# Local attention scores on TensorE as 64x64 products instead of 128x128 ones, with a new order of steps

## The chip, the cores and the metric

One core of a Trainium2 chip. The metric is device time in microseconds of one execution; the lower the better. TensorE is called PE here, VectorE DVE, ScalarE ACT, GpSimd POOL and SyncE SP, as in the profile. SP issues all loads and stores of this kernel.

## What is computed

Attention over 2 batches of 8 heads, 768 positions and 64 channels, then two feed-forward layers on the 1536 tokens of 512 channels, all in float32.

```python
k_sum = k.reshape(B, H, nb, block, D).max(axis=3)          # block = 32, nb = 24
v_sum = v.reshape(B, H, nb, block, D).mean(axis=3)
mask_l = np.abs(pos[:, None] - pos[None, :]) < window      # window = 16
scores_s = scale * np.einsum('bhsd,bhnd->bhsn', q, k_sum) + np.log(block)
scores_l_m = np.where(mask_l, scale * q @ k.T, -1000000000.0)
a = softmax over concatenate([scores_l_m, scores_s], axis=-1)
x = a @ np.concatenate([v, v_sum], axis=2)
x = np.maximum(x @ w_in, 0.0) ** 2 @ w_out
h = x @ w_in2
out = np.where(h >= 1, h, np.where(h <= -1, 0.0, (h + 1) ** 2 / 4)) @ w_out2
```

A query of the local part sees only the keys within 15 positions, so a tile of 64 queries needs 96 keys around it and the 24 block maxima: 120 columns of scores.

## The kernel before

**Attention** is cut into 24 units. A unit i is a chunk of 256 positions (6 chunks, 3 per batch) and a pair of heads (4 pairs); `geo` (line 301) gives them. Its steps have one letter each in the written order: S the scores on PE (`s_mm`, line 337), M the mask added to them and the minimum of the negated sums (`s_max`, 344, on DVE), E the exponentials (`s_exp`, 353, ACT), R the reciprocal of the sums (`s_inv`, 359), N the product with it (`s_norm`, 364, POOL or DVE), T the transpose on PE (`t_mm`, 368), "to" its way out of PSUM (`t_out`, 373), O the product with v (`o_mm`, 376), oh and ol the high and low part of the result (`o_hi`, `o_lo`), which fill `xh` and `xl`, the input of the feed-forward part.

S of a unit is 4 products of 128 rows and 128 columns. The rows are the channels of both heads; q is loaded into a tile with zeros in the other head's places, and one product takes 128 weight columns of it, 64 queries of each head, at every fourth element (`bass.ds(j, 128, step=4)`). The moving side is a tile `kw` of 24 block maxima, 8 empty columns and 96 keys, four times (for the 4 tiles of 64 queries). For the first 4 units `kw_band` (327) copies the keys into it out of `kp`; for the other 20 SP loads it ready-made (`kw_load`, 321), and `kw_sum` (333) copies the block maxima that `k_sum` (324) made on DVE. The fills of lines 456 to 462 clear the empty parts of kw, q and vw.

```python
PE.matmul(ps[:, j * 128:(j + 1) * 128], qs[cc % 2][:, p, bass.ds(j, 128, step=4)],
          kw[i % NW][:, j, :], start=True, stop=True)
```

The block means of v for batch 0 are products on PE (v0 to v2, vc, vj: `v_sum0`, `v_copy0`, `v_join0`, lines 402 to 413) of a table of weights with v, both loaded by `vn_load` (437); for batch 1 DVE adds them (`v_sum1`).

**Feed-forward.** The 16 weight slices of each layer come as packed 64-bit numbers of 512 KB per half (wl, `w_load`, line 128) and are decoded into a high and a low part by steps on ACT, DVE and POOL (dl, dq, dr, ds, dt, da, wh, wo; lines 132 to 162). A unit of this part is one slice of 128 hidden channels for one tile of tokens: H (`h_mm`, 186) is 12 products into PSUM, ha, hh, hl the activation and its split into high and low, Y (`y_mm`, 225) 12 products more, yo the way out. The first 24 units take tiles of 256 tokens, so that they can begin when a part of the attention is done; the other 84 take 512.

**Order.** Each engine runs its instructions in the order of the program and waits only for what an instruction needs. That order is written out by hand in a string of steps (`PLAN`, line 83): all of attention, the 24 small units, and the decoding up to weight half 15. After it a loop (line 484) takes the rest in a regular order, from unit 24 (`UA`) on: activation of unit u+1, H of u+2, Y of u, one weight half decoded.

Of the kernel before, what the change touches and what calls it, by code (L numbers as in the profile page):

```python
# [43 lines left out]
KW = QT + 2 * WIN  # L44
NGRP = NCH * NP
# [7 lines left out]
CONST_W = M_OFF + 6 * 128  # L53
SUM_W = 6 * 32 + NB
# [23 lines left out]
Y0 M8 N6g E8 wl3 da4 ks9 wo4g S9 kwl11 vs0 M9 E7 R7 N7g kl6 wl5 vl2 wo1v O4 oh4v ol4 T6 to6a ks11 R8 dq3 dr3 S10 E9 O5
oh5v N8g kwl12 ol5 H1 ha1 R9 O6 T7 to7a vp0 M10 S11 E10 oh6v ol6 O7 T8 ds3 dt3 kl7 N9g hh1v dl3 da3 M11 E11 oh7v ol7
H2 to8v T9 ha2 R11 O8 oh8a kl4 km4 H3 hh2a to9a hl1g ol8 O9 kwl13 R10 N10g kwl14 ks12 kl5 km5 wl6 H4 dq6 wh3v dq5 hl2v  # L80
ha4 wo3v Y1 dr6 N11v kwl15 dl5 Y2 ql3 T10 S12 H6 hh4a oh9a ol9 dr5 ds5 km6 ks14 to10a O10 ks13 T11 dl6 dt5 wh5a wl7
M12 S13 da5 wo5v oh10v ha3 hh3a ds6 dt6 da6 wh6v dq7 ol10 H5 hl3v bl1 M13 vs1 to11a O11 oh11a ol11 wl8 vl3 ql4 hl4g
dr7 Y3 ha6 hh6v ha5 S14 kwl18 M14 wo6g Y4 H7 km7 ks15 vp1 vf3 E12 R12 N12g ds7 dl7 E14 kwl16 E13 R13 N13g hh5v S15 M15
T12 dt7 H8 da7 hl6v Y6 dl8 ha8 to12a H10 kwl17 ks16 E15 R15 kwl19 T13 O12 wl9 oh12a wh7v wo7v hl5g N15v R14 to13v ha7
S16 ol12 M16 Y5 yo5 ks17 N14v kwl20 hh7v hl7g H9 ha9 T14 to14v hh9v S17 hh8v E16 R16 hl8v H11 O13 T15 M17 ks18 hl9v
oh13v vl4 S18 ol13 to15v O14 ql5 ha11 M18 ks19 oh14v ol14 kwl22 N16g T16 dq8 vf4 kwl21 ha10 E17 R17 Y7 N17v E18 to16v
O15 oh15v R18 Y8 Y9 dq9 dr9 T17 N18g hh10a ol15 O16 dr8 ds8 S19 vl5 M19 E19 dl9 oh16v kwl23 H12 hl10g Y10 to17v T18
# [9 lines left out]
"""  # L97


def build(tc, qd, kd, kwd, vw, vn, vb, wd, cd, out):  # L100
    nc = tc.nc
    V, A, G, PE, SY = nc.vector, nc.scalar, nc.gpsimd, nc.tensor, nc.sync

# [3 lines left out]
    with tc.tile_pool(name="main", bufs=1) as mp, tc.tile_pool(name="ps", bufs=1, space=PSUM) as pp:  # L107
# [213 lines left out]
        def kw_load(i):  # L321
            SY.dma_start(kw[i % NW], kwd[i - NP])
# [287 lines left out]
```

## Time and profile before

| | us |
|---|---|
| median of 3 runs (lowest to highest) | 627.0 (626.37 to 631.27) |
| the profiled execution | 630.58 |
| its span, first to last instruction | 628.8 |

The profiled execution is one of its own; what is said of single instructions comes from it. Its mean granted clock of PE is 0.992 of full speed. Busy shares of an engine say how long it had an instruction in it, not that it could not have done more. A matmul in fp32 stands in the trace as two records, each with its own weight load (PEld); records overlap, so the time of a group is read from the start of one group to the start of the next.

### The profile page before, as it was taken

How to read it: one execution, taken by the hardware profiler on the slowest of the kernel's cores; microseconds unless marked ns; L12 is line 12 of the kernel's file. 1: busy time of each engine (PE TensorE's matmuls, PEld its weight loads, DVE VectorE, ACT ScalarE, POOL GpSimd, SP SyncE). 2: the span in 40 equal slices, each digit the busy share in tenths (PEclk: the TensorE clock that was granted, in tenths of full speed). 3: DMA queues.
4: the chain of work that ended last, by engine and by line, in shares of the span. 5: the costliest groups of instructions: out<-in, count | busy, mean ns of one | idle time of the engine just before them, and what ended most of it. 6: DMA issues, size and time to landing. Idle time of an engine off the chain costs nothing.

```text
span 628.8 us, 9073 instructions
## 1 busy us (share of the span) xinstructions
PE 612.2 (97%) x3301; PEld 521.1 (83%) x3301; DVE 353.9 (56%) x806; ACT 309.9 (49%) x674; POOL 271.4 (43%) x225
## 2 busy tenths in 40 slices
PE   7789899999999999999999999999999999999997
PEld 5488899999888888888888888888888888888886
DVE  7787767557555545545457665443555545653343
ACT  3866476476564444444354555554544354432221
POOL 4353231246542331343155666554655565552211
PEclk8898999999999999999999999999999999999999
DMA  8999956412321211132022213211222211100111
GB/s 293 295 220 262 237 141 162 127 35 70 104 87 48 96 67 35 67 102 68 33 68 67 68 34 102 66 61 40 68 67 68 70 67 68 33 1 0 68 67 68
DMA packets 20765, 58.13 MB, mean 92 GB/s; under 512 B 2416, under 2 KB 5968, under 8 KB 19952
## 3 DMA queue, kind: packets, MB, share of 16 engines
q1 hardware_dynamic: 20720, 57.55, 31.1%
q8 instruction: 26, 0.43, 0.3%
q14 instruction: 19, 0.16, 0.1%
HBM read 53.65 MB, written 3.15 MB: 90 GB/s over the span
## 4 chain that ended last, share of the span: by engine, by line
PE 74%; DVE 0%; issue 0%
PE bank L198 37%; PE bank L237 35%; PE bank L519 2%; DVE acc L523 0%
## 5 line engine op out<-in xcount | busy, mean ns | idle before, releaser
L149 POOL TENSOR_TENSOR fr<-fx,fr 128x512 uint32<-128x512 uint32 x64 | 83.3, 1302 | 186.7 <-DVE fx L146 172.4
L198 PE MATMUL bank<-xh,wh 128*128 128x512 f32 (+1 forms) x432 | 156.2, 369 | 0.0
L198 PE MATMUL bank<-xl,wh 128*128 128x512 f32 (+1 forms) x432 | 155.0, 366 | 0.3 <-DVE xl L395 0.3
L222 POOL TENSOR_TENSOR gl<-tb,gh 128x512 fp32r<-128x512 f32 (+1 forms) x62 | 72.6, 1171 | 101.4 <-ACT gh L218 77.5
L198 PE MATMUL bank<-xh,wl 128*128 128x512 f32 (+1 forms) x432 | 105.2, 365 | 0.0
L198 PEld LDWEIGHTS bank<-xl,wh 128*128 128x128 f32 x432 | 81.5, 189 | 13.6 <-DVE xl L395 0.5
L198 PEld LDWEIGHTS bank<-xh,wh 128*128 128x128 f32 x432 | 81.5, 189 | 13.4
L198 PEld LDWEIGHTS bank<-xh,wl 128*128 128x128 f32 x432 | 76.3, 189 | 13.1
L159 ACT CAST wh<-fx 128x512 fp32r<-128x512 f32 x57 | 35.4, 621 | 98.0 <-DVE fx L146 96.6
L162 POOL TENSOR_TENSOR wl<-fr,wh 128x512 fp32r<-128x512 f32 x58 | 76.1, 1312 | 5.8 <-ACT wh L159 0.9
L215 DVE CAST gh<-tb 128x512 fp32r<-128x512 f32 (+1 forms) x49 | 24.4, 501 | 93.5 <-ACT tb L207 88.8
L237 PE MATMUL bank<-gh,wh 128*128 128x512 f32 (+1 forms) x240 | 62.3, 351 | 0.5 <-DVE wh L159 0.5
L237 PE MATMUL bank<-gl,wh 128*128 128x512 f32 (+1 forms) x240 | 61.5, 348 | 0.6 <-DVE gl L222 0.5
L206 ACT ACTIVATE ta<-bank 128x512 f32<-128x512 f32 (+1 forms) x60 | 30.6, 510 | 63.6 <-PE bank L198 63.6
L237 PE MATMUL bank<-gh,wl 128*128 128x512 f32 (+1 forms) x240 | 61.1, 346 | 0.0
L210 ACT ACTIVATE ta<-ta,bias 128x512 f32<-128x512 f32 x48 | 34.8, 724 | 49.6 <-DVE ta L209 49.6
L209 DVE TENSOR_SCALAR ta<-bank 128x512 f32<-128x512 f32 x48 | 33.0, 687 | 44.1 <-PE bank L198 44.1
L142 DVE TENSOR_SCALAR fx<-fx 128x512 f32<-128x512 f32 x64 | 29.7, 465 | 45.9 <-ACT fx L140 45.6
L218 ACT CAST gh<-tb 128x512 fp32r<-128x512 f32 x48 | 29.9, 624 | 49.7 <-DVE tb L217 49.7
L341 PE MATMUL bank<-kw,q 128*128 128x128 f32 x192 | 49.3, 409 | 4.9 <-DMA q<-in_qd_dram 4.6
L217 DVE SCALAR_TENSOR_TENSOR tb<-bank,ta 128x512 f32<-128x512 f32 x48 | 33.1, 690 | 34.7 <-ACT ta L210 17.4
L237 PE MATMUL bank<-wh,gh 128*128 128x512 f32 x176 | 52.4, 389 | 0.0
(75 smaller groups left out, 985.5 us busy)
## 6 DMA issues: line engine op xcount, KB each, us to landing
raw<-in_wd_dram SPq DMA_DIRECT2D x64, 512.0 KB
kw<-in_kwd_dram SPq DMA_DIRECT2D x20, 256.0 KB
vw<-in_vw_dram SPq DMA_DIRECT2D x6, 768.0 KB
k<-in_kd_dram SPq DMA_DIRECT2D x8, 400.0 KB
q<-in_qd_dram SPq DMA_DIRECT2D x12, 256.0 KB
out_dram<-acc SPq DMA_DIRECT2D x11, 256.0 KB
acc<-in_vb_dram SPq DMA_DIRECT2D x2, 768.0 KB
acc<-in_vn_dram SPq DMA_DIRECT2D x2, 512.0 KB
```

Of the source, the lines that this page charges most:

```text
L149: G.tensor_tensor(fr[n % NDEC], fx[n % NDEC], fr[n % NDEC], ALU.add)
L159: cp(e)(w_part(wh, n), f32(fx[n % NDEC]))
L162: e.tensor_tensor(w_part(wl, n), f32(fr[n % NDEC]), f32(w_part(wh, n)), ALU.subtract)
L198: PE.matmul(h, a, b, start=i == 0, stop=i == len(ops) - 1)
L206: A.activation(a, h, AF.Relu)
L209: V.tensor_scalar(a, h, -1.0, 1.0, ALU.max, ALU.min)
L210: A.activation(a, a, AF.Square, bias=bias[:, 1:2], scale=0.5)
L217: V.scalar_tensor_tensor(b, h_bank(n), 1.0, a, ALU.max, ALU.mult)
L218: A.copy(hi, b)
L222: e.tensor_tensor(lo, b, f32(hi), ALU.subtract)
L237: PE.matmul(ys[j], a, b, start=f == 0 and i == 0 and (tw == 512 or j % 2 == 0), stop=f == GF - 1 and i == 2 and (tw == 512 or j % 2 == 1))
L341: PE.matmul(ps[:, j * 128:(j + 1) * 128], qs[cc % 2][:, p, bass.ds(j, 128, step=4)], kw[i % NW][:, j, :], start=True, stop=True)
```

## The change

- **Scores.** q is loaded dense, keys are read where they lie in `kp` and block maxima in `ks`; there is no kw any more. A unit is 16 products in fp32: for each of two halves t, 4 products with 96 keys and 4 with 24 maxima, one for each head h (rows 0 to 63 or 64 to 127 of the array) and query tile r (columns 0 to 63 or 64 to 127). The two heads write different PSUM banks (`sbank`). A unit's scores are 120 columns wide instead of 128: keys first, then maxima.
- **Constants and buffers.** Three masks of 128 columns instead of six, all 8 k tiles stay in place (4 buffers before), v has a third buffer in `acc`.
- **Block means of v, batch 0.** 12 products of 96 rows out of the v tiles themselves; the table is 128x96 numbers.
- **PSUM.** Small units from 12 on write their H into banks 4 and 3 in turn; Y of small tiles uses banks 2 and 3 for t = 1 alone.
- **Order.** A new string of steps, which goes four units further (the loop begins at unit 28) and decodes up to weight half 18.

```diff
+KN = KW + NB
...
-CONST_W = M_OFF + 6 * 128
-SUM_W = 6 * 32 + NB
+CONST_W = M_OFF + 3 * 128
+Z_W, SUM_W = 64, 96
...
-kl1 kb1a ql0 kl0 kb0a km1 ks1 warm11 km0 ks0 kl3 km3 ks3 kb3v cl0 S1 M1 E1 kl2 kb2v wl0 S0 wl1 km2 S3 nl2 ks2 S2 R1
+kl1 ql0 warm11 km1 S1 cl0 M1 E1 kl3 km3 S3 wl1 dl1 kl0 km0 S0 dq1 dr1 ql1 M3 S5 ds1 kl2 km2 R1 N1g wl0 dt1 da1 dl0 T1
...
-                ybank[m, g, t] = [bank[2 * (t % 2) + j // 2][:, j % 2 * CH:(j % 2 + 1) * CH] for j in range(4)]
+                ybank[m, g, t] = [bank[2 * (t == 1) + j // 2][:, j % 2 * CH:(j % 2 + 1) * CH] for j in range(4)]
...
         def h_bank(n):
+            if n < 3 * GF:
+                return bank[4][:, n % 2 * CH:(n % 2 + 1) * CH]
             if U[n][3] == CH:
-                return bank[4][:, n % 2 * CH:(n % 2 + 1) * CH]
+                return bank[4 - n % 2][:, :CH]
             return bank[4 + n % 2]
...
-        NK, NW, NS, NPT = 4, 4, 4, 3
+        NK, NS, NPT = B * NP, 4, 3
         cst = av.tile([128, CONST_W], F32, name="cst")
-        qs = [at.tile([128, NP, 2 * CH], F32, name=f"q{i}") for i in range(2)]
+        qs = [at.tile([128, NP, CH], F32, name=f"q{i}") for i in range(2)]
...
-        kw = [at.tile([128, 4, 128], F32, name=f"kw{i}") for i in range(NW)]
...
+        vwt.append(acc[:, 2048:4096].rearrange("p (j n) -> p j n", j=4))
+        vwt += [vwt[0], vwt[1], vwt[0]]
...
+        def sbank(i, j):
+
+            if i < 8:
+                b = ((5, 1), (2, 3))[i % 2][j // 2]
+                c0 = CH * (b != 5)
+            else:
+                b = (5, 2 if i < 10 or i > 15 else 6)[j // 2]
+                c0 = CH * (i % 2 or b == 6)
+            c0 += j % 2 * 128
+            return bank[b][:, c0:c0 + KN]
...
         def q_load(cc):
-            for hf in range(2):
-                SY.dma_start(qs[cc % 2][hf * 64:hf * 64 + 64, :, hf * CH:(hf + 1) * CH], qd[cc, hf])
+            SY.dma_start(qs[cc % 2], qd[cc])

         def v_load(cc):
-            SY.dma_start(vwt[cc % 2][32:128], vw[cc])
+            SY.dma_start(vwt[cc][:KW], vw[cc])
...
-        def kw_load(i):
-            SY.dma_start(kw[i % NW], kwd[i - NP])
...
-        def kw_band(i, e=A):
+        def s_mm(i):
+
             cc, p, c, n = geo(i)
-            base = kp[n % NK][:, c * CH:c * CH + KW]
-            cp(e)(kw[i % NW][:, :, 32:128], bass.AP(base.tensor, base.offset, [list(base.ap[0]), [QT, 4], [1, KW]]))
-
-        def kw_sum(i):
+            for t in range(2):
+                for keys in (True, False):
+                    for h in range(2):
+                        for r in range(2):
+                            j, rows = 2 * t + r, slice(h * 64, h * 64 + 64)
+                            k0 = c * CH + j * QT
+                            b = kp[n % NK][rows, k0:k0 + KW] if keys else ks[n][rows]
+                            PE.matmul(sbank(i, 2 * h + t)[r * 64:r * 64 + 64, 0 if keys else KW:KW if keys else KN],
+                                      qs[cc % 2][rows, p, j * QT:(j + 1) * QT], b, start=True, stop=True)
...
-                PE.matmul(ps[:, j * 128:(j + 1) * 128], qs[cc % 2][:, p, bass.ds(j, 128, step=4)],
-                          kw[i % NW][:, j, :], start=True, stop=True)
...
-                m0 = M_OFF + (c + j) * 128
-                V.tensor_tensor_reduce(s[:, j, :], ps[:, j * 128:(j + 1) * 128], cst[:, m0:m0 + 128],
+                m0 = M_OFF + (0 if (c, j % 2) == (0, 0) else 2 if (c, j % 2) == (CPB - 1, 1) else 1) * 128
+                V.tensor_tensor_reduce(s[:, j, :KN], sbank(i, j), cst[:, m0:m0 + KN],
                                        -SCALE, 3.0e38, ALU.add, ALU.min, st[:, j:j + 1])
...
-                    rs = slice(hf * 64, hf * 64 + 64)
-                    PE.matmul(ps[rs, j * QT:(j + 1) * QT], vwt[cc % 2][:, j, p * 128 + hf * 64:p * 128 + hf * 64 + 64],
-                              pt[i % NPT][:, j, rs], start=True, stop=True)
+                    rs, r0 = slice(hf * 64, hf * 64 + 64), j % 2 * QT
+                    PE.matmul(ps[rs, j * QT:(j + 1) * QT], vwt[cc][:KN, j, p * 128 + hf * 64:p * 128 + hf * 64 + 64],
+                              pt[i % NPT][:KN, 2 * hf + j // 2, r0:r0 + QT], start=True, stop=True)
...
-            for c in (2 * k, 2 * k + 1):
-                rs = slice(c % 4 * 32, c % 4 * 32 + 32)
-                PE.matmul(bank[0][rs], vx[:, c * 32:(c + 1) * 32], vx[:, SUM_W + c * 512:SUM_W + (c + 1) * 512],
-                          start=c < 4, stop=c >= 2)
+            for j in range(4):
+                b0 = NB - 8 * k - 2 * j
+                PE.matmul(bank[0][j * 32:j * 32 + 32], vx[:KW, b0:b0 + 32], vwt[k][:KW, j], start=k == 0, stop=k == 2)
...
-        for w in kw:
-            G.memset(w[:, :, 0:32], 0.0)
-        for q in qs:
-            for hf in range(2):
-                (V if q is qs[0] else G).memset(q[hf * 64:hf * 64 + 64, :, (1 - hf) * CH:(2 - hf) * CH], 0.0)
-        for w in vwt:
-            G.memset(w[:32], 0.0)
...
-        nd = nl = 4 * GF
-        h_mm(UA + 1)
+        nd, nl = 5 * GF - 1, 5 * GF - 2
+        h_mm(UA + GF + 1)
         last = len(U) - GF
-        for u in range(UA, last):
+        for u in range(UA + GF, last):
...
-    qd = q.reshape(B, NP, 2, CPB, 4, QT, D).transpose(0, 3, 2, 6, 1, 5, 4)
-    qd = np.ascontiguousarray(qd.reshape(NCH, 2, D, NP, CH))
+    qd = q.reshape(B, NP, 2, CPB, CH, D).transpose(0, 3, 2, 5, 1, 4)
+    qd = np.ascontiguousarray(qd.reshape(NCH, 2 * D, NP, CH))
```

How the instructions stand now. The first place is PE in the first third of the attention, around the second chunk's score units. Names are tiles with a running number; L341 and L348 are the score products, L382 and L390 the products with v, L371 and L379 the transposes. Before:

```order
L382 MATMUL bank_64<-pt_132,vw_134 64x64 x8
L371 MATMUL bank_70<-cst,s_129 128x128 x4
L341 MATMUL bank_68<-kw_124,q_110 128x128 x4
L382 MATMUL bank_65<-pt_133,vw_134 64x64 x8
L341 MATMUL bank_68<-kw_125,q_110 128x128 x4
L382 MATMUL bank_66<-pt_131,vw_134 64x64 x8
L371 MATMUL bank_70<-cst,s_127 128x128 x4
L341 MATMUL bank_68<-kw_126,q_110 128x128 x4
```

After:

```order
L390 MATMUL bank_66<-pt_131,vw_134 64x64 x8
L390 MATMUL bank_65<-pt_133,vw_134 64x64 x8
L379 MATMUL bank_70<-cst,s_127 120x128 x4
L348 MATMUL bank_68<-k_111,q_109 64x96 x2
L348 MATMUL bank_65<-k_111,q_109 64x96 x2
L348 MATMUL bank_68<-ks_119,q_109 64x24 x2
L348 MATMUL bank_65<-ks_119,q_109 64x24 x2
L348 MATMUL bank_68<-k_111,q_109 64x96 x2
L348 MATMUL bank_65<-k_111,q_109 64x96 x2
L348 MATMUL bank_68<-ks_119,q_109 64x24 x2
L348 MATMUL bank_65<-ks_119,q_109 64x24 x2
L390 MATMUL bank_69<-pt_132,vw_135 64x64 x8
```

A row of 4 products with kw became 8 rows of 2 products each: keys into two banks, maxima into the same two, and once more for the other half; "x2" are the two query tiles of one head.

The second place is the beginning of SP's queue, where all loads are issued (raw is a weight half, vn the table of block means with v, cst the constants). Before:

```order
L308 DMA k_112<-in_kd_dram 128x800
L312 DMA q_109<-in_qd_dram 64x4x256 x2
L308 DMA k_111<-in_kd_dram 128x800
L308 DMA k_114<-in_kd_dram 128x800
L434 DMA cst<-in_cd_dram 128x640
L308 DMA k_113<-in_kd_dram 128x800
L130 DMA raw_74<-in_wd_dram 128x1024
L130 DMA raw_75<-in_wd_dram 128x1024
L438 DMA acc<-in_vn_dram 128x1024
L438 DMA acc<-in_vn_dram 128x1240
L438 DMA acc<-in_vn_dram 128x1024
L322 DMA kw_123<-in_kwd_dram 128x512
```

After:

```order
L325 DMA q_109<-in_qd_dram 128x1024
L441 DMA cst<-in_cd_dram 128x384
L322 DMA k_114<-in_kd_dram 128x800
L131 DMA raw_75<-in_wd_dram 128x1024
L322 DMA k_111<-in_kd_dram 128x800
L325 DMA q_110<-in_qd_dram 128x1024
L322 DMA k_113<-in_kd_dram 128x800
L131 DMA raw_74<-in_wd_dram 128x1024
L328 DMA vw_134<-in_vw_dram 96x2048
L444 DMA acc<-in_vn_dram 128x96
L328 DMA vw_135<-in_vw_dram 96x2048
L328 DMA acc<-in_vw_dram 96x2048
```

The three loads of vn and the loads of kw are gone, q comes in one load, and vw stands three times in the first thirteen places (the third one, the last row, writes acc).

The third place is DVE at the program's start (L325 and L335 of after are the block maxima, L335 and L331 of before the copies into kw). Before:

```order
L460 MEMSET q_109 64x4x256 x2
L325 TENSOR_REDUCE ks_116<-k_112 128x24
L335 COPY kw_124<-ks_116 128x4x24
L325 TENSOR_REDUCE ks_115<-k_111 128x24
L335 COPY kw_123<-ks_115 128x4x24
L325 TENSOR_REDUCE ks_118<-k_114 128x24
L335 COPY kw_126<-ks_118 128x4x24
L331 COPY kw_126<-k_114 128x4x96
```

After:

```order
L297 MEMSET acc 128x256
L335 TENSOR_REDUCE ks_120<-k_112 128x24
L357 ISA s_128,sm_139<-bank_65,cst 128x120
L357 ISA sm_139 128x1
L357 ISA s_128,sm_139<-bank_65,cst 128x120
L357 ISA sm_139 128x1
```

Between a block maximum and the first score no copy stands any more.

## Rows read from the trace of the kernel before

**Rows 1.** The page, busy time, share of the span and instructions of each engine

```profile
PE 612.2 (97%) x3301; PEld 521.1 (83%) x3301; DVE 353.9 (56%) x806; ACT 309.9 (49%) x674; POOL 271.4 (43%) x225
```

**Rows 2.** Four stretches: us, busy time (instructions) by engine, clock, DMA share, GB/s

```profile
0.00:25.00 25.00, 17.48 (x85) 11.38 (x85) 18.26 (x64) 13.30 (x44) 9.96 (x16) 0.93 0.95 284
25.00:80.00 55.00, 49.83 (x421) 46.02 (x422) 42.91 (x159) 32.73 (x108) 22.41 (x20) 0.94 0.98 250
80.00:164.20 84.20, 83.46 (x736) 80.44 (x735) 54.57 (x190) 55.01 (x179) 33.14 (x31) 1.00 0.38 108
164.20:628.80 464.60, 461.44 (x2064) 383.22 (x2063) 238.11 (x394) 208.82 (x345) 205.91 (x159) 1.00 0.19 61
```

**Rows 3.** The chain that ended last, from 176 us: start us, us, what

```profile
176.69 2.72 PE bank L237 x12
179.41 2.72 PE bank L198 x12
```

**Rows 4.** What PE waited for: us in total, times, longest us

```profile
PE bank L341 <- DMA q<-in_qd_dram: 4.6, 3, 2.3
PE bank L371 <- POOL s L366: 2.0, 2, 1.4
PE bank L382 <- DMA vw<-in_vw_dram: 1.5, 1, 1.5
...
PE bank L382 <- DMA vw<-vs: 0.6, 1, 0.6
```

**Rows 5.** Groups of lines on PE: names, shapes, count | busy us, mean ns

```profile
L341 PE MATMUL bank<-kw,q 128*128 128x128 f32 x192 | 49.3, 409 | 4.9 <-DMA q<-in_qd_dram 4.6 <-DVE sm L350 0.3
L341 PEld LDWEIGHTS bank<-kw,q 128*128 128x128 f32 x192 | 46.5, 327 | 6.4 <-issue 2.8 <-DMA q<-in_qd_dram 1.4 <-ACT pt L374 1.1
...
L382 PE MATMUL bank<-pt,vw 128*64 128x64 f32 x384 | 17.3, 236 | 3.2 <-DMA vw<-in_vw_dram 1.5 <-DVE vw L417 1.1 <-DMA vw<-vs 0.6
...
L371 PEld LDWEIGHTS bank<-cst,s 128*128 128x128 f32 x96 | 11.2, 148 | 4.0 <-POOL s L366 2.4 <-DVE fx L142 0.8
...
L413 PE MATMUL bank<-acc 128*24 128x512 f32 x2 | 1.0, 601 | 0.7 <-ACT acc L410 0.7
```

**Rows 6.** PE in order of time, 0 to 60 us: start us, us, what

```profile
8.00 7.84 PE L341 MATMUL bank<-kw,q 128*128 128x128 f32 x32 [2.35 <-DMA q<-in_qd_dram]
...
18.24 1.91 PE L406 MATMUL bank<-acc 128*32 128x512 f32 x12
20.86 1.04 PE L413 MATMUL bank<-acc 128*24 128x512 f32 x2 [0.72 <-ACT acc L410]
...
40.27 2.02 PE L341 MATMUL bank<-kw,q 128*128 128x128 f32 x8
42.12 0.60 PE L371 MATMUL bank<-cst,s 128*128 128x128 f32 x4
...
54.18 0.69 PE L382 MATMUL bank<-pt,vw 128*64 128x64 f32 x16
54.79 0.66 PE L371 MATMUL bank<-cst,s 128*128 128x128 f32 x4
```

**Rows 7.** Groups of lines on DVE, by busy time

```profile
L146 DVE SCALAR_TENSOR_TENSOR fx<-raw,fx 128x512 uint32<-128x512 uint32 x64 | 46.1, 720 | 2.0
...
L144 DVE TENSOR_SCALAR fx<-fx 128x512 uint32<-128x512 uint32 x64 | 30.5, 477 | 1.9
...
L142 DVE TENSOR_SCALAR fx<-fx 128x512 f32<-128x512 f32 x64 | 29.7, 465 | 45.9 <-ACT fx L140 45.6
...
L335 DVE COPY kw<-ks 128x96 f32<-128x96 f32 x24 | 7.4, 314 | 6.4 <-DMA kw<-in_kwd_dram 6.0
```

**Rows 8.** DMA issues: names, count, KB each

```profile
kw<-in_kwd_dram SPq DMA_DIRECT2D x20, 256.0 KB
...
acc<-in_vn_dram SPq DMA_DIRECT2D x2, 512.0 KB
acc<-in_vn_dram SPq DMA_DIRECT2D x1, 620.0 KB
```

More of the change, by code (lines that the diff above doesn't have):

```diff
@@ L78 @@
[L78 to L87, printed above, removed]
@@ L97, with build @@
+hh23a hl23v dt15 wh15a wl18 Y22 wl17 ds16 dt16 wh16a H27 ha27 hh27a Y23 yo23 hl24g H26 ha26 hh26v hl26g Y24 Y25 hl27g
+da16 wo16v da15 wo15v dl18 dq18 dr18 dl17 Y26 ds18 dq17 dr17 dt18 da18 H28 wl19 ds17 dt17 wl20 da17 ha28 Y27 hh28v
+hl28v wh17a wo17g wl21
 """
-def build(tc, qd, kd, kwd, vw, vn, vb, wd, cd, out):
+def build(tc, qd, kd, vw, vn, vb, wd, cd, out):
     nc = tc.nc
@@ L259, in y_out @@
                     A.copy(av[:, :, t % 2 * CH:(t % 2 + 1) * CH],
-                           bank[2 * (t % 2) + j // 2].rearrange("p (j n) -> p j n", j=2))
+                           bank[2 * (t == 1) + j // 2].rearrange("p (j n) -> p j n", j=2))
                 return
@@ L303, in abank @@
         def abank(kind, i):
-            first = {"s": (5, 1, 2, 3), "t": (7, 6, 7, 5), "o": (6, 1, 2, 3)}
-            return bank[first[kind][i] if i < 4 else {"s": 5, "t": 7, "o": 6}[kind]]
+            first = {"t": (7, 6, 7, 5), "o": (6, 1, 2, 3)}[kind]
+            return bank[first[i] if i < len(first) else {"t": 7, "o": 6}[kind]]
+        def sbank(i, j):
[7 more added lines that the diff above has]
+            return bank[b][:, c0:c0 + KN]
         def k_load(n):
@@ L412, in v_join0 @@
         def v_join0(_):
-            PE.matmul(bank[0][:NB], vx[:, 6 * 32:SUM_W], vq, start=True, stop=True)
+            PE.matmul(bank[0][KW:KN], vx[:, Z_W:Z_W + NB], vq, start=True, stop=True)
         def v_fill0(p, e):
@@ L558, in host @@
             vw[cc, :, j] = vt[b, s0:s0 + KW]
-            kw[cc, :, :, j, 32:] = kd[b * NP:(b + 1) * NP, :, s0:s0 + KW]
-    kw = kw.reshape(NGRP, 2 * D, 512)[NP:]
-    vn = np.zeros((128, SUM_W + 6 * H * D), v.dtype)
-    for s in range(S):
-        vn[s % 128, s // 128 * 32 + s // BLK] = 1.0 / BLK
+    vn = np.zeros((128, SUM_W), v.dtype)
     for p in range(128):
+        if 0 <= p - WIN < QT:
+            vn[p, NB + (p - WIN) // BLK] = 1.0 / BLK
         if p % 32 < NB:
-            vn[p, 6 * 32 + p % 32] = 1.0
-    vn[:, SUM_W:] = vt[0, WIN:WIN + S].reshape(6, 128, H * D).transpose(1, 0, 2).reshape(128, -1)
+            vn[p, Z_W + p % 32] = 1.0
     vb = v[1].reshape(2, 4, NB, BLK, D).transpose(0, 1, 2, 4, 3)
@@ L582, in consts @@
     c[:, I_OFF:I_OFF + 128] = np.eye(128, dtype=np.float32)
-    qi = np.arange(128)[:, None] % QT
+    qi = np.arange(QT)[:, None]
     w = np.arange(KW)[None, :]
     band = np.abs(qi - (w - WIN)) < WIN
-    for i in range(6):
-        ok = band & ((w >= WIN) | (i > 0)) & ((w < KW - WIN) | (i < 5))
-        m = c[:, M_OFF + i * 128:M_OFF + (i + 1) * 128]
-        m[:, :NB] = np.log(BLK) / SCALE
-        m[:, NB:32] = NEG
-        m[:, 32:] = np.where(ok, 0.0, NEG)
+    for i in range(3):
+        for r in range(2):
+            ok = band & ((w >= WIN) | ((i, r) != (0, 0))) & ((w < KW - WIN) | ((i, r) != (2, 1)))
+            m = c[r * QT:(r + 1) * QT, M_OFF + i * 128:M_OFF + i * 128 + KN]
+            m[:, :KW] = np.where(ok, 0.0, NEG)
+            m[:, KW:] = np.log(BLK) / SCALE
     return c
```

72 lines of the change are left out of this document (36 added, 36 removed).

## The prediction

> **What bounds the kernel now.** Read the engines' share first [rows 1]: TensorE (PE) is busy 97% of the span, VectorE (DVE) 56%, ScalarE 49%. A busy matmul engine can still be one that waits inside its work, so the stretches come next [rows 2]. There the run has two parts. From 164.2 us to the end PE is busy 461.4 of 464.6 us, and the chain of waits shows why nothing else matters there [rows 3]: groups of 12 products of 512 columns follow each other every 2.72 us, product after product, without a wait. One unit of the feed-forward part costs two such groups, 5.44 us, and the change leaves the number of these units and of their products alone. So this part is a constant, and the time is decided by the moment at which PE gets there. In the first 164.2 us PE is busy 17.5 of 25, 49.8 of 55 and 83.5 of 84.2 us: it idles for 13.4 us, nearly all of it before 80 us, where the DMA queues are full (0.95 and 0.98 of their time) and DVE is busy 42.9 of 55 us. Who PE waited for there is in the table of waits [rows 4]: q loads 4.6 us, loads of vw 1.5 and 0.6 us, 2.0 us for the normalised scores of GpSimd (POOL), the rest under 1.5 us each.
>
> The groups of lines tell what fills PE in the front part [rows 5]. The 192 records of the score products (line 341) hold 49.3 us, more than any other attention line, although the 96 transposes of line 371 move the same 128 columns against weights of the same 128x128 shape. The difference stands in the weight loads: 327 ns each for line 341, 148 for line 371. Line 341 takes its weights from q at every fourth element. In order of time [rows 6] a score unit of 8 records begins at 40.27 and the next group at 42.12, 1.85 us or 231 ns per record, while the 4 transposes that follow take 0.60 us with all of their last record, at most 150 ns per record. PE spends more than half of a score unit on loading weights slowly.
>
> **The change part by part.** *Score products.* Removed: 24 units of 4 products of 128x128, 24 x 1.85 = 44.4 us. Added: 24 units of 16 products, each with 64 rows and 64 weight columns: 8 over 96 keys and 8 over 24 block maxima, in two halves of 4 + 4, one product per quarter of the array. q now lies dense. No row shows products on half of the rows, so the cost is bounded. Two rows give the parts. The two records of line 413 (512 columns, fp32) take 1.04 us [rows 6] with 0.60 for the last [rows 5], so 0.44 us per 512 columns, 0.86 ns a column: 96 keys are 0.083 us per record, and a product has two records. The 16 records of line 382 (64 weight columns, two products side by side on the two column halves) take 0.69 us [rows 6] with 0.24 for one [rows 5], so 15 steps in 0.45 us: 30 ns each, or 0.060 us per record on its own half; the next group starts 0.61 us after the first record, so the last record and the change-over to another shape of the array cost 0.61 - 0.45 = 0.16 us. Hence, for a unit:
> - four at a time: per half 2 x 0.083 for the keys and 2 x 0.060 for the maxima, 0.286; two halves 0.57; with the change-over 0.73 us.
> - at the pace of line 382, 30 ns for each of 32 records: 0.96 + 0.16 = 1.12 us.
> - two at a time (column halves side by side, row halves in turn): twice 0.57, with the change-over 1.30 us.
> - one at a time: four times 0.57, with the change-over 2.45 us, more than before.
>
> I take 0.92, the middle of the first two: line 382 is the nearest row, and it shows that products on separate parts of the array do run side by side. Saving 24 x (1.85 - 0.92) = 22.3 us; ends 26.9 (0.73) and -14.4 (2.45).
>
> What a page says of this pace stands apart. The Trainium skill, TensorE: Matmul & The Clock Gate, section "Wait — 56ns, not 53.3ns?", says that starts of matmuls never come closer than about 25 ns, however few columns they have. The trace's closest steady pace is the 30 ns above. By the page's figure a unit would be an estimated 32 x 0.025 + 0.16 = 0.96 us and the sum below 1.0 us longer; by the row's 30 ns it would be 4.8 us longer.
>
> *Copies and loads that go.* The 24 copies of block maxima into kw on DVE (7.4 us), 4 copies of key bands and 10 fills go [rows 7], as do 20 loads of kw (256 KB) and three of vn (512, 512, 620 KB) against one small one [rows 8]: 6.9 MB of the 20.9 MB that the queues move in the first 80 us (284 GB/s over 25 us, 250 over 55) [rows 2]. At those rates that is some 25 us of queue time, taken out of the stretch where the queues are full. q arrives in one load of whole rows instead of two. PE's waits for loads in this part are 4.6 + 1.5 + 0.6 = 6.7 us [rows 4]. The bounds are 0 and -6.7; I count half, -3.4, because the first loads (k, q, before 8.00 us [rows 6]) can't come earlier and because two vw loads now stand earlier in the queue.
>
> *Block sums of v.* Before: 6 products of 128 rows and 512 columns, 12 records in 1.91 us [rows 6]. Now 12 products of 96 rows, 4 column quarters at a time: 3 rounds of 2 records of 0.44 us, 2.6 us. +0.7 us (0 to +1.9), and PE has to have three vw loads instead of the vn loads.
>
> *Start.* The four first score units run from 8.00 us on for 7.84 us [rows 6], with the first transposes right behind them. When they shrink to 3.7 us, PE gets to the transposes early and waits for the first unit's maximum, exponentials, reciprocal and POOL's product, so part of their saving (4 x 0.93 = 3.7) turns into a wait. I count half as lost: +2.0 (0 to +3.7). The granted clock is 0.93 and 0.94 of full speed in the first two stretches and 1.00 behind them [rows 2], some 1.8 + 3.3 = 5 us of clock lost; a PE that waits more at the start could lose more of it, and I leave this term at 0 with the same loss once more, +5, as its end.
>
> *The order.* Steps of four more feed-forward units now stand in the written order, and three more weight tiles are decoded ahead of the loop (3 x (465 + 477 + 720) ns = 5.0 us of DVE [rows 7]). PE's products in these units are the same and PE has no idle time behind 164.2 us [rows 2], so this is worth 0 as long as PE's queue hides it. Ends: 0 if hidden, +5.0 if DVE is late by all of it.
>
> *Narrower tiles.* Maxima, exponentials and products of scores work on 120 instead of 128 columns. They lie beside PE's work and count 0.
>
> Sum: -22.3 - 3.4 + 0.7 + 2.0 = -23.0 us. The profiled execution took 630.6 us (span 628.8 and 1.8 around it) and would take 607.6; it lies 3.6 us over the median of the runs, 627.0. Against the median the forecast is 627.0 - 23.0 = 604, and I write 603.5 because the DMA term is the one more likely to be larger.
>
> **The rivals.**
> 1. *The row halves don't overlap.* A unit costs 1.30 us; the saving is 24 x 0.55 = 13.2, and with the other terms (4 x 0.55 / 2 at the start) 627.0 - 13.2 - 3.4 + 0.7 + 1.1 = 612. For it: no product of this kernel has used half the rows. Against it: the halves write different PSUM banks, and the column halves of line 382 do overlap.
> 2. *DVE becomes the bound of the front part.* From 25 to 164.2 us DVE is busy 42.9 + 54.6 = 97.5 us [rows 2]. Less the copies of kw behind 25 us (about 5.5) and plus the decoding (5.0) it is 97. With 23 us gone from PE that has to fit into 116 us, a share of 84%; between 25 and 80 us DVE reached 78%. If 78% is what its waits allow, 97 / 0.78 = 124 us are needed, 8 us more: 612. For it: DVE is the fullest of the others just where PE idles. Against it: the order hands copies to ScalarE and POOL, which are under 60%.
> 3. *The quarters run one after another, the kernel gets slower.* Every product holds the array alone: 2.45 us per unit, 24 x 0.60 = 14.4 us more on PE, less 3.4 for the loads, plus 0.7: 639. It decides from 1.85 + 2.7 / 24 = 1.96 us per unit on, that is when the 16 products take more than 0.12 us each. For it: 64 loads and products per unit instead of 16, and an array that changes its shape twice per unit. Against it: line 382.
>
> The Trainium skill speaks to this one: TensorEngine Tiling (Array Packing), section "Gotcha 1: PSUM Pressure", says that different row tiles can't reach the same PSUM bank at once. No row here shows it; the new placing has the row halves in different banks, so by that rule one reason for rivals 1 and 3 is gone; at the lower end that this leaves, 0.73 us per unit, the sum would give 599.
>
> **How the numbers follow.** Forecast 0.70, rival 1 0.14, rival 2 0.10, rival 3 0.06. The forecast's own range is from 596 (0.73 us per unit, nothing lost at the start: 627.0 - 26.9 - 3.4 + 0.7 = 597, and a little more of the waits for loads gone) to 610 (1.12 us: 604 + 24 x 0.20, and the rest of the start, 1.7). Rivals 1 and 2 at 612, with 3 or 4 us of their own, are taken in: 596 to 616; rival 3 and some of the tails stay out. About 1% (6 us) is what a measurement of this kernel tells from no change. Forecast, rival 1 and most of rival 2 are faster by more than that: 0.91. Rival 2 with all its terms on the bad side, or rival 3 between 1.7 and 2.2 us per unit, is no change: 0.05. The rest of rival 3 is slower: 0.04.
>
> **What would show it.** Right: the start of the steady groups of 2.72 us moves from about 164 to about 141 us; a score unit starts its next group 0.7 to 1.1 us after its own first record; the dense weight loads are far under 327 ns; PE's waits for q and vw shrink and the share of the queues in the first 80 us falls under 0.9; the stretch behind the front lasts as long as before. Wrong: score units at 1.3 us or more (rival 1, from 1.96 on rival 3); idle time of PE between 25 and 140 us released by DVE or ScalarE that is larger than now (rival 2); a gap in the steady part, which would mean that the moved decoding was not hidden.

## The result, and the profile after

| | before | after |
|---|---|---|
| median of 4 runs (lowest to highest), us | 627.7 (626.37 to 631.27) | 607.71 (605.38 to 608.92) |
| the profiled execution, us | 630.58 | 605.38 |
| its span, us | 628.8 | 603.5 |

After stands to before as 0.967, 95% interval 0.962 to 0.972: 20 us less by the medians. The two profiled executions lie 25.2 us apart, because that of before is among its slowest runs and that of after is its fastest; a sum read from the one trace has to be held against the other, so against 25.2.

The page of after, busy time and share of the span of each engine, against [rows 1]:

```profile
PE 589.2 (98%) x3889; PEld 493.4 (82%) x3889; DVE 345.4 (57%) x779; ACT 309.1 (51%) x672; POOL 262.5 (43%) x214
```

The stretches of after (us, busy time by engine with instructions, clock, DMA share, GB/s), the third cut where the steady groups were forecast to begin, and the chain of waits of after behind it:

```profile
0.00:25.00 25.00, 17.80 (x227) 10.51 (x231) 14.74 (x71) 12.22 (x47) 4.29 (x8) 0.70 0.94 280
25.00:80.00 55.00, 51.17 (x818) 44.10 (x814) 47.78 (x169) 44.19 (x147) 29.64 (x28) 0.98 0.71 211
80.00:141.00 61.00, 61.00 (x801) 57.91 (x796) 46.53 (x153) 44.50 (x136) 22.60 (x20) 1.00 0.23 72
141.00:603.50 462.50, 459.18 (x2057) 380.89 (x2056) 236.36 (x389) 208.22 (x344) 205.98 (x160) 1.00 0.18 61
```

```profile
161.53 2.72 PE bank L201 x12
164.25 2.72 PE bank L240 x12
```

Set beside [rows 2, 3], the back part is the same: groups of 2.72 us, PE busy 459 of 462.5 us. The first product of unit 31 stands 25.4 us earlier than before, and so does that of the last unit (587.73 against 613.09 us). All of the gain was made before that. The first product of unit 30 stands at 195.57 us before and at 169.53 after, 26.0 us earlier, of which 0.7 is lost again up to unit 31. Up to unit 30 (before, then after):

```profile
0.00:195.57 195.57, 182.15 (x1394) 164.52 (x1394) 133.20 (x441) 118.13 (x359) 80.06 (x77) 0.97 0.60 167
```

```profile
0.00:169.53 169.53, 158.50 (x1982) 137.07 (x1982) 123.60 (x411) 116.18 (x355) 69.73 (x66) 0.95 0.49 150
```

PE's busy time fell by 23.7 us and its idle time by 2.4 (13.4 to 11.0). What it waits for has changed more. PE's table of waits of after (us in total, times, longest us):

```profile
PE bank L379 <- POOL s L374: 2.0, 2, 1.6
PE bank L348 <- DVE sm L357: 1.8, 2, 1.1
PE bank L379 <- DVE sm L357: 1.5, 1, 1.5
...
PE bank L348 <- DMA k<-in_kd_dram: 0.7, 1, 0.7
```

The 6.7 us for q and vw of [rows 4] are gone, and one load is left, with 0.7 us. The waits for DVE rose instead, from 4.0 to 6.7 us in all, 3.3 of them for the maxima; the whole table fell from 13.4 to 10.5 us.

The groups of lines on PE of after (names, shapes, count | busy us, mean ns | idle before), to compare with [rows 5], and PE in order of time, against [rows 6]:

```profile
L348 PE MATMUL bank<-k,q 64*64 64x96 f32 x384 | 18.3, 284 | 2.9 <-DVE sm L357 1.8 <-DMA k<-in_kd_dram 0.7 <-ACT pt L382 0.4
...
L348 PEld LDWEIGHTS bank<-ks,q 64*64 64x64 f32 x384 | 13.2, 150 | 1.4 <-DVE ks L335 1.4
```

```profile
18.84 1.94 PE L414 MATMUL bank<-vw,acc 96*32 96x512 f32 x8
...
40.63 0.40 PE L348 MATMUL bank<-k,q 64*64 64x96 f32 x8
40.85 0.26 PE L348 MATMUL bank<-ks,q 64*64 64x24 f32 x8
40.93 0.38 PE L348 MATMUL bank<-k,q 64*64 64x96 f32 x8
41.13 0.26 PE L348 MATMUL bank<-ks,q 64*64 64x24 f32 x8
41.32 0.69 PE L390 MATMUL bank<-pt,vw 120*64 120x64 f32 x16
```

A weight load of the scores takes 150 ns (327 before). A score unit lasts from 40.63 to 41.32, 0.69 us in place of 1.85; its two halves start 0.30 us apart, and 0.28 where two units follow each other.

### The profile page after: what moved, and what is told of

The parts are those of the page before. It is cut to its first block, busy times and chain, and to the rows that moved or that the text cites. A ratio compares the mean times of both kernels' runs of the same rounds, so it can differ in the third digit from the quotient of the medians.

```text
span 603.5 us, 10148 instructions
## 1 busy us (share of the span) xinstructions
PE 589.2 (98%) x3889; PEld 493.4 (82%) x3889; DVE 345.4 (57%) x779; ACT 309.1 (51%) x672; POOL 262.5 (43%) x214
## 4 chain that ended last, share of the span: by engine, by line
PE 90%; DVE 4%; DMA 3%; ACT 1%; SPq 1%; issue 0%; DVEq 0%
PE bank L201 42%; PE bank L240 41%; PE bank L517 2%; DMA raw<-in_wd_dram 2%; DMA acc<-in_vb_dram 2%; PE bank L348 1%; PE bank L379 1%; PE bank L390 1%; DVE vt L431 1%; PE bank L414 1%; DVE fx L147 0%; ACT s L363 0%; DVE s L357 0%; DVE xl L403 0%; DVE gh L218 0%
## 5 line engine op out<-in xcount | busy, mean ns | idle before, releaser
L225 POOL TENSOR_TENSOR gl<-tb,gh 128x512 fp32r<-128x512 f32 (+1 forms) x64 | 76.1, 1190 | 105.7 <-ACT gh L221 77.4
L163 POOL TENSOR_TENSOR wl<-fr,wh 128x512 fp32r<-128x512 f32 x56 | 73.1, 1306 | 5.7 <-DVE wh L160 2.0
L209 ACT ACTIVATE ta<-bank 128x512 f32<-128x512 f32 (+1 forms) x60 | 30.5, 509 | 51.2 <-PE bank L201 51.2
L240 PE MATMUL bank<-wh,gl 128*128 128x512 f32 x176 | 52.4, 389 | 0.0
```

Source lines behind the costliest of these rows:

```text
L163: e.tensor_tensor(w_part(wl, n), f32(fr[n % NDEC]), f32(w_part(wh, n)), ALU.subtract)
L209: A.activation(a, h, AF.Relu)
L225: e.tensor_tensor(lo, b, f32(hi), ALU.subtract)
L240: PE.matmul(ys[j], a, b, start=f == 0 and i == 0 and (tw == 512 or j % 2 == 0), stop=f == GF - 1 and i == 2 and (tw == 512 or j % 2 == 1))
```

## The experiments

Each kernel was timed beside the kernel before on the same chip; ratios are to that, with their 95% interval. The theories go by letters in the expectations, which are not the same in all of them.

**1. Dense weights alone.** The kernel before, with q read densely (queries then meet keys of other tiles; the work is the same in kind and number):

```diff
-                PE.matmul(ps[:, j * 128:(j + 1) * 128], qs[cc % 2][:, p, bass.ds(j, 128, step=4)],
+                PE.matmul(ps[:, j * 128:(j + 1) * 128], qs[cc % 2][:, p, j * 128:(j + 1) * 128],
```

> The kernel before, in which each score product takes 128 neighbouring weight columns of q instead of every fourth; which queries meet which keys changes, everything else (loads, copies, order, counts) stays. Theory A (the gain is TensorE's time in the score products, whatever its cause): the weight load falls from 327 to about 148 ns, a unit from 1.85 to about 0.9 us, 24 x 0.95 = 23 us go and the time is 605 to 610 us. Rival B (the loads have to be relieved as well): the unit falls as far, but TensorE then waits for q, vw and kw in the first 80 us, where the queues stay full; 614 to 621 us. If the stride is not the cause, the unit stays at 1.85 us and the time at 627.

Measured: 620.32 us, ratio 0.986 (0.980 to 0.991). The weight loads shrink, and the units at full clock with them, to between 0.8 and 1.0 us:

```profile
L341 PEld LDWEIGHTS bank<-kw,q 128*128 128x128 f32 x192 | 26.7, 214 | 10.9 <-DVE sm L350 2.2 <-DMA q<-in_qd_dram 2.0 <-DVE kw L335 2.0
```

But PE then waits. Its table of waits in this kernel:

```profile
PE bank L341 <- DVE kw L335: 3.9, 4, 1.4
PE bank L382 <- DMA vw<-in_vw_dram: 2.6, 1, 2.6
PE bank L382 <- DMA vw<-vs: 2.1, 1, 2.1
```

With the copies and loads of before and its order, some 9 of the 22 us that PE saves reach the end.

**2. The new kernel in the order of before.** Products, loads, narrow tiles and block means of v as after; the string of steps of before without the steps that fell away, the v loads and sums moved to where their data can be there, the loop from unit 24, the small feed-forward units in the PSUM places of before.

> The changed kernel (64x64 scores, dense q, no kw) with the order of steps of the kernel before; only the steps of kw are left out, M0, M2 and the three first v loads are moved as far as the new banks and the new block means need it, the small units keep their old PSUM banks and the loop starts at unit 24 as before. Theory A (products, not order): within 3 us of the changed kernel, 605 to 611 us. Rival C (the new order carries a good part of the gain): 615 to 622 us. In between, both carry.

Measured: 630.47 us, ratio 1.003 (1.000 to 1.007). No gain is left. Part of that is the block means: in this order the v sums wait for the v tiles, and the first feed-forward product comes at 45.9 us (38.8 before).

**3. The new score products alone.** To take that part away: the kernel before, its order and its block means of v, with the products of after, keys and maxima read where they lie, no kw.

```diff
-kl1 kb1a ql0 kl0 kb0a km1 ks1 warm11 km0 ks0 kl3 km3 ks3 kb3v cl0 S1 M1 E1 kl2 kb2v wl0 S0 wl1 km2 S3 nl2 ks2 S2 R1
+kl1 ql0 kl0 km1 warm11 km0 kl3 km3 cl0 S1 M1 E1 kl2 wl0 S0 wl1 km2 S3 nl2 S2 R1 N1g
...
```

(In this order S of unit 2 overwrites the scores of unit 0 before their maxima are taken, so unit 0 works with the scores of unit 2. The score tiles stay 128 wide: the products with the maxima have 32 columns, 8 of them empty.)

> The kernel before with the new score products alone (keys and block sums read where they lie, no copied windows, no 256 KB loads, queries loaded without zeros); the block sums of v, the 128-wide tiles and the order of steps (without the steps that fell away) stay as before. Theory A (the prediction's sum: each microsecond off the score units and the loads comes off the time, order worth 0): 24 units of 1.85 fall to 0.69 us (27.8 us) and the loads give 0 to 6.7, so 594 to 603 us. Theory B (before, the front is held by loads, VectorE and the chains between the steps as much as by TensorE, so the old order cannot use the time that TensorE gains; dense weights alone gave 9 us of some 22): 612 to 622 us. Theory C (the old order gives nothing back at all, as the run with the block sums of v changed too seemed to say): 625 to 632 us.

Measured: 625.0 us, ratio 0.9945 (0.991 to 0.998): 1.7 us by the medians, 3.4 by the ratio. Its stretch from 25 to 80 us, PE's waits, and PE in order of time:

```profile
25.00:80.00 55.00, 44.30 (x628) 38.90 (x629) 40.61 (x152) 32.77 (x109) 20.68 (x19) 0.81 0.65 186
```

```profile
PE bank L386 <- DVE sm L354: 5.1, 2, 3.1
PE bank L386 <- DVE xl L399: 2.6, 4, 1.1
PE bank L375 <- POOL s L370: 2.3, 2, 1.2
```

```profile
43.97 0.38 PE L345 MATMUL bank<-k,q 64*64 64x96 f32 x4
46.13 0.42 PE L345 MATMUL bank<-k,q 64*64 64x96 f32 x2 [1.77 <-DVE xl L399]
```

The loads are no longer in the way (share 0.65), yet PE is busy only 44.3 of 55 us, against 49.8 before and 51.2 after. PE and DVE wait for each other: DVE for PE's scores (6.4 us, 6 times, from 30 to 141 us; 8.8 before, 1.9 after), and PE for DVE's maxima and copies (15.5 us in all, 4.0 before). The wait at 46.13 is one in the middle of a unit, for a copy of an earlier result. A score unit reads only k, maxima and q, so it can only have waited for its PSUM bank, which in the kernel before no result shares: part of this loss may lie in the new PSUM places, for which the old order was not written. The granted clock is 0.81 in this stretch, so that much of what PE still does runs at the lower of its two levels, 1.2 GHz. Up to the first product of unit 30, which stands at 189.41 us here:

```profile
0.00:189.41 189.41, 167.80 (x1970) 144.06 (x1970) 122.61 (x413) 117.29 (x357) 77.63 (x79) 0.92 0.47 144
```

Against the kernel before PE's idle time rose from 13.4 to 21.6 us. Its busy time fell by 14.4 us, not by the 28 that the units save; the clock up to there is 0.92 against 0.97. Of the 28 us, 6 are left in the profiled execution.

**4. Two and three times the score products, in the new order.**

```diff
-            for t in range(2):
+            for t in (0, 1) * 3:
```

(`* 2` for two issues.)

> The changed kernel with each score unit's 16 products issued twice: 0.65 us more of TensorE for each of 24 units, 15.6 us in all. With three issues the time rose by 36 us where 31 us of products were added, and TensorE's row showed 18 us of waits that nothing released (issue). If the units lie on the path one for one in the new order: 607.7 and 15.6, so 620 to 626 us, with few such waits. If the first 15 us hide behind other engines and only more than that is felt: 608 to 614 us.

> The changed kernel with each score unit's 16 products issued three times (the last result counts, which is the same one): a unit then takes about 2.0 us in place of 0.69, near the 1.85 of the kernel before, with the new loads, copies, sums and order kept. Theory A (each microsecond of the units is on the path): 24 times 1.3 is 31 us more, 638 us. Theory B (the front has slack outside TensorE, so that part of it is hidden; rows in turn gave 2.7 us of 7): 615 to 628 us. Theory C (the units are not on the path, order and loads made the gain): under 612 us.

Measured: 622.14 us with two issues, ratio 0.990 (0.985 to 0.994), and 643.9 us with three, 1.025 (1.021 to 1.030). A unit at full clock lasts 1.25 and 1.81 us, so 0.56 us for each issue and 0.13 around it. The one of 1.81, from its first group to the first one behind it:

```profile
71.99 0.40 PE L348 MATMUL bank<-k,q 64*64 64x96 f32 x8
...
73.80 0.69 PE L390 MATMUL bank<-pt,acc 120*64 120x64 f32 x16
```

PE's waits that nothing released, with two issues and with three:

```profile
PE bank L348 <- issue: 6.1, 3, 2.8
...
PE bank L390 <- issue: 0.6, 1, 0.6
```

```profile
PE bank L348 <- issue: 14.8, 6, 6.6
PE bank L379 <- issue: 3.0, 2, 2.4
```

The spans grew by 13.4 and 40.0 us. Products give 24 x 0.56 = 13.4 and 24 x 1.12 = 26.9, the waits for issue 6.7 and 17.8; PE's waits for other engines fall from 10.5 to 4.3 and 4.2 us. 13.4 + 6.7 - 6.2 = 13.9, and 26.9 + 17.8 - 6.3 = 38.4. So in the new order some 6 us of PE's time hide behind other engines, and all the rest is on the path one for one. The waits for issue belong to this experiment: PE has none in the changed kernel. Less 17.8 us of them, the new order with units as long as before (1.81 us) would take an estimated 626 us, no less than the kernel before, although the loads of kw are gone from it.

**5. Row halves in turn.** The changed kernel with the loop over heads outside, so that the two row halves of the array work one after the other:

```diff
-            for t in range(2):
-                for keys in (True, False):
-                    for h in range(2):
+            for h in range(2):
+                for t in range(2):
+                    for keys in (True, False):
```

> The changed kernel with the loops of the score products turned round: all 8 products of the first head (rows 0 to 63), then all 8 of the second, so that only the two column halves can be side by side. If four at a time is what happens: a unit goes from 0.69 to about 1.2 us, 24 x 0.5 = 12 us more on TensorE, of which the first units are hidden: 614 to 620 us. If the row halves do not overlap in the changed kernel either: the unit stays at 0.69 us and the time at 605 to 609 us.

Measured: 608.39 us, ratio 0.967 (0.963 to 0.972), span 606.2. PE in order of time:

```profile
46.08 0.38 PE L348 MATMUL bank<-k,q 64*64 64x96 f32 x4
...
47.07 0.69 PE L390 MATMUL bank<-pt,vw 120*64 120x64 f32 x16
```

A unit takes 0.99 us in place of 0.69 for the same products, so in the changed kernel the row halves do overlap. Of the 7.2 us more on PE, PE's waits take up 3.8 (10.5 to 6.7), and the span grows by 2.7: the slack of experiment 4 again.

**6. The four units further.** The new string cut where that of before ends, the loop from unit 24 on.

> The changed kernel with its written order ended where that of the kernel before ends (the 45 steps of the four units further left to the loop that follows, which then starts four units earlier). Theory A (the four units are worth nothing, as the order was priced): 607 to 609 us. Theory D (they carry a part of the gain, the start of unit 28 moves later): 611 us or more.

Measured: 607.7 us, ratio 0.968 (0.964 to 0.972), the time of the changed kernel. These steps are worth nothing.

**7. The loads put back.** 20 loads of 256 KB into tiles that nothing reads, first with two tiles, then with four for the first fourteen (two of these lie in `acc`; there is no room for four more tiles):

```diff
+        def x_load(i):
+            SY.dma_start(xt[i % 2], xd[i])
...
```

> The changed kernel with 20 loads of 256 KB into two tiles that nothing reads put back on the queue, near the times at which the kernel before issued its window loads. If the prediction's load term is right (3.4 us, 0 to 6.7) 611 us (608 to 614.5). If the queue has so much room after the change that volume costs nothing, 608 us and no wait for a transfer over 1 us on TensorE. If volume is what held the front of the kernel before, 615 us or more, with waits for q, k or vw back.

> As the run with 20 loads of 256 KB put back, but with four tiles for the first fourteen loads in place of two (the kernel before had four), so that the queue's own waits for a free tile, 25 us of them in that run, mostly go and volume alone is left. If the 12.6 us of that run were volume (queue share in 25 to 80 us up from 0.71, waits of TensorE for vw): 616 to 621 us. If they were the queue standing behind loads that waited for a tile: 608 to 613 us, near the prediction's 3.4 us.

Measured: 620.27 us with two, ratio 0.987 (0.984 to 0.990); 616.49 us with four, 0.978 (0.971 to 0.985). The stretch from 25 to 80 us, PE's waits for loads and DVE's with four tiles:

```profile
25.00:80.00 55.00, 48.06 (x723) 39.96 (x716) 40.80 (x149) 39.10 (x127) 26.14 (x25) 0.87 0.76 240
```

```profile
PE bank L400 <- DMA vw<-in_vw_dram: 2.4, 1, 2.4
PE bank L358 <- DMA k<-in_kd_dram: 2.4, 2, 2.1
```

```profile
DVE ks L345 <- DMA k<-in_kd_dram: 8.5, 5, 3.4
```

With two tiles SP stood 25.5 us behind loads that waited for a tile, with four 12.0. So of 12.6 us some 4 go with the tiles, and 8.8 by the medians (7 by the ratios, from runs between 612.3 and 618.9 us) are left, for 5.2 of the 6.9 MB that the change took out. Not only PE waits for loads: DVE waits 8.5 us for k in the first 80 us where it waited 4.2 without them, and its maxima, and the exponentials behind them, come later. Since some waiting for tiles is left in it, volume alone may be less than 8.8.

**8. The copies put back.** 20 copies of block maxima (128x4x24) on DVE, one ahead of each unit from unit 4 on.

```diff
+        def kw_sum(i):
+            cc, p, c, n = geo(i)
+            V.tensor_copy(kw[:, :, 0:NB], ks[n].unsqueeze(1).to_broadcast([128, 4, NB]))
...
```

> The changed kernel with 20 copies of a block-sum tile over four windows (128x4x24, 0.31 us of VectorE each in the kernel before) put back on VectorE, one ahead of the maxima of each unit from unit 4 on, written to a tile that nothing reads: 6.3 us of VectorE. If VectorE is the bound of the front behind TensorE (87% busy from 25 to 80 us after the change): 611 to 614 us. If its rest is slack: 607 to 609 us.

Measured: 608.33 us, ratio 0.966 (0.959 to 0.972). DVE is busy 50.5 of 55 us from 25 to 80 us, 92%, and nothing is lost that stands out from the scatter: what was left of its time there was slack.

**9. Filling the start.** 22 products of zeros in the gaps of the first 30 us:

```diff
-kl1 ql0 warm11 km1 S1 cl0 M1 E1 kl3 km3 S3 wl1 dl1 kl0 km0 S0 dq1 dr1 ql1 M3 S5 ds1 kl2 km2 R1 N1g wl0 dt1 da1 dl0 T1
...
+kl1 ql0 warm11 km1 S1 warm4 cl0 M1 E1 kl3 km3 S3 warm3 wl1 dl1 kl0 km0 S0 warm2 dq1 dr1 ql1 M3 S5 warm7 ds1 kl2 km2 R1 N1g wl0 dt1 da1 dl0 T1
...
```

> The changed kernel with 22 more filler products (bf16, 512 columns, into a bank that nothing uses yet) in the places where TensorE waits in the first 22 us: 4 behind the first score unit, 3, 2 and 7 behind the next three, 6 behind the first block means. Theory D (the start is lost to the clock): the granted clock of the first 25 us rises from 0.70 to over 0.9, a record of the block means falls from 0.85 to 0.43 us, and the time falls by 3 to 5 us to 602 to 605. Rival E (TensorE is not the bound there, it waits for DVE, loads and POOL anyway): the clock rises as well, the time stays within 1.5 us of the changed kernel, 606 to 609 us.

Measured: 607.31 us, ratio 0.965 (0.961 to 0.969). The first stretch of this kernel:

```profile
0.00:25.00 25.00, 18.62 (x237) 9.31 (x241) 12.69 (x60) 11.54 (x45) 3.70 (x7) 0.88 0.94 270
```

The granted clock there rose from 0.70 to 0.88, the second and third round of v sums fell from 1.94 and 1.63 to 1.06 and 1.07 us, and the time did not move. That does not show PE to be off the path. The chain of waits of the changed kernel runs over PE from 22.32 us on, through transposes and v sums:

```profile
22.32 1.93 PE bank L379 x8
24.25 3.32 PE bank L414 x16
27.59 0.59 ACT acc L417
28.23 1.05 PE bank L420 x2
```

That of the kernel with fillers runs over the fillers, which stand there ahead of the same transposes:

```profile
22.23 2.34 PE bank L408 x5
24.57 0.23 PE bank L379
```

So the fillers took what the sums gave back, and the first feed-forward product came at 39.99 us (38.48 in the changed kernel). What the lower clock of the start costs stays open.

**10. The old block means of v in the new kernel.** 1.6 MB of v on 128 partitions ahead of the first v tile, six products, the second and third v tile loaded behind them.

```diff
-                PE.matmul(bank[0][j * 32:j * 32 + 32], vx[:KW, b0:b0 + 32], vwt[k][:KW, j], start=k == 0, stop=k == 2)
+                PE.matmul(bank[0][rs], vx[:, c * 32:(c + 1) * 32], vx[:, SUM_W + c * 512:SUM_W + (c + 1) * 512],
+                          start=c < 4, stop=c >= 2)
...
```

> The changed kernel with the block sums of v of batch 0 as before: 1.6 MB of v loaded for them on 128 partitions in three loads ahead of the first v window, six products of 128 rows in place of twelve of 96, and the second and third v windows loaded once the sums are done. If the prediction's terms for the sums and the start are right (0.7 and 2.0 us): 605 us. If the first 38 us are held by loads and the chains beside TensorE whatever the sums are: 606.5 to 609 us. If the 1.5 MB more in that stretch are felt: 610 us or more.

Measured: 611.28 us, ratio 0.973 (0.970 to 0.976): 3.6 us more. The means are ready earlier (their last product at 24.42 us in place of 28.23), but then PE stands still, by its table of waits:

```profile
PE bank L390 <- DMA vw<-vs: 5.5, 1, 5.5
PE bank L348 <- DMA q<-in_qd_dram: 2.2, 1, 2.2
```

The fill of block means for the second chunk and a q load stand in the queue behind v tiles that now come later. So the new sums cost nothing that the old ones, placed like this, would save; a better place for the old ones was not tried.

No run was clearly faster than the changed kernel; experiment 9, the lowest, lies within its scatter.

## Why the prediction was right, and where its reasons were not

The time, 607.7 us, lies in the range and 4 us above the predicted 603.5; in the profiled executions the sum of -23.0 us met -25.2. "Faster" was right. The steps one by one:

- *What bounds the kernel* held: the back part is a constant, and the signs named for it came: no waits for q and vw, queue share 0.71 from 25 to 80 us (in the first 25 us it stayed at 0.94), and groups of 2.7 us from 139 us on, with some of 1.44 us between them up to 150.5, because the written order goes further.
- *Score products*, -22.3: the direction was right, the size too small. 0.69 us per unit is just under the lower bound of 0.73: two halves of 0.28 (0.286 was worked out) and 0.13 (not 0.16) for the change-over. That is 24 x 1.16 = 27.8 us of PE. The choice of 0.92 failed: the pace of line 382, 30 ns per record, is no limit; 16 records of a half take 0.28 us, 17.5 ns each. (By the prediction's own figures a record of line 382 takes 0.060 us on its half, and two halves side by side give the 30 ns; that says nothing of how closely records can start.) The figure of 25 ns from the Trainium skill's TensorE: Matmul & The Clock Gate, "Wait — 56ns, not 53.3ns?", by which a unit would have taken an estimated 0.96 us, is not borne out by the records of products that run side by side on quarters of the array.
- *The order*, 0. As it was worded, about four units further, it is right (experiment 6). But the sum took for granted that a microsecond off PE comes off the time whatever the order, and that is what failed. In the old order the same products, with the loads of kw gone too, are worth 2 to 3 us (experiment 3), in the new one what is added to PE counts, but for some 6 us, and by estimate the new order with long units gains nothing (experiment 4). Neither part has a price of its own; the 20 us belong to the two together. The old order with the new products was run as it stands, not fitted again by hand, and its PSUM places differ from the changed kernel's for the scores from unit 16 on and for the small feed-forward units, so how much lies in the order of steps and how much in the places stays open.
- *Copies and loads*, -3.4 with an end at -6.7: too small. The bound was taken from PE's waits for loads alone; experiment 7 gives about 7 to 9 us, with the scatter named there, for three quarters of the volume, and in it DVE waits longer for k as well. The copies that went with the loads are worth nothing (experiment 8). The volume was misread, too: 8 of the 20 loads of kw were issued behind 82 us, so that some 4.8 MB, not 6.9, left the first 80 us. SP in the kernel before:

```profile
59.69 0.38 SPq L322 DMA_DIRECT2D kw<-in_kwd_dram  x1
...
82.50 0.34 SPq L322 DMA_DIRECT2D kw<-in_kwd_dram  x1
```

- *Block sums of v*, +0.7, and *start*, +2.0: PE's part of the sums was under-counted. They run while PE is at 1.2 GHz, 1.94 us in two of the three rounds, and hold PE about 5.3 us against 1.91; they stand on the chain of waits (experiment 9). The clock of after in this stretch (a granted clock of 0.50 is 1.2 GHz):

```profile
15.00:17.00 2.00, 1.67 (x24) 1.34 (x28) 1.41 (x13) 1.56 (x5) 1.51 (x2) 0.50 1.01 236
...
24.00:27.00 3.00, 3.00 (x18) 0.55 (x16) 1.71 (x7) 2.10 (x9) 1.26 (x1) 0.50 1.04 377
```

What the sums cost in time no run shows: experiment 10 is slower for another reason. The start lost all that its score units saved, not half: the first feed-forward product comes at 38.48 us against 38.76, with two more score units done by then. The clock term was 0 with an end of +5. The granted clock did fall (0.93 to 0.70), and whether at a price stays open (experiment 9).

- *Narrower tiles*, 0: not tried by itself.
- *Rival 1* falls by experiment 5 and its unit of 0.99 us; it would have cost 1 to 3 us and not 8, since the row halves in turn take 0.3 us more, not 0.6. (The heads wrote different PSUM banks in all runs with the new products, so that the rule of the Trainium skill's TensorEngine Tiling (Array Packing), "Gotcha 1: PSUM Pressure", was not tested.) *Rival 2* falls, although the sign named for it came: from 25 to 140 us PE's idle time released by DVE or ACT rose from 0.8 to 3.1 us. But DVE is busy 87% from 25 to 80 us, and 92% in experiment 8 without a loss; the 78% that it reached before was no limit. In the old order, though, DVE and PE do wait for each other (experiment 3). *Rival 3* falls by the unit's 0.69 us.

So the sum came close in part by luck: two mis-sized gains (units 5 us, loads perhaps as much) stood against what the start swallowed and the slack of some 6 us that the new order leaves.

## What to carry to other kernels

When a step on the busiest engine becomes nearly three times shorter, price the order as a part of the change: the long step was also the cover under which others got ready, and in an order made for the long step the gain turns into waits and a lower clock. To see what a shorter step is worth, lengthen it in the finished kernel: issued twice and three times it showed both the price per microsecond and the slack. And bound the worth of a load by the waits of all engines that need its data, not by those of the last one.

## What the runs showed of the hardware beyond what was expected

- Sixteen fp32 products of 64 rows and 64 weight columns, on four quarters of the array, take 0.56 us, eight with 96 moving columns and eight with 24 (0.28 per half of 16 records), 0.13 us more with a change of shape; with the row halves in turn 0.86 (experiment 5).
- A weight load of 128 columns from every fourth element took 327 ns, from neighbouring ones in the same kernel 214 ns (experiment 1); one of 64 dense columns 150 ns.
- PE's clock: with PE busy 17.8 of the first 25 us the granted clock was 0.70 there; with fillers (18.6 of 25, shorter gaps) 0.88. At 1.2 GHz (0.50 from 15 to 17 us) the four transposes that take 0.65 us elsewhere took 1.11.
- With 384 and 768 more products in the program PE stood still for 6.7 and 17.8 us with nothing in the profile that released it. Its instructions came late, as the packets of the instruction queue q8 in the traces tell: 16 KB each, 30 in the changed kernel, 36 and 42 here, and each of these 12 waits ended 1.2 to 1.6 us after the end of one (the longest, 16.03 to 22.63 us with three issues, after a packet from 19.64 to 21.08). Why those packets came no earlier is not shown; the load queues were 0.94 busy in the first 25 us, where the two longest waits of two issues and the longest of three fall.
